# A decode attention and gMLP kernel under one critical section: recorded waits, a TensorE loop over 28 quads, one identity load per 16 matmuls

## The chip, the cores and the metric

The kernel runs on one core of a Trainium2 chip (trn2). The metric is device time in microseconds, in the median of several executions. Before the change it is 667.79 us, the median of three runs (667.62 to 667.85).

## The reference, cut to what matters

One decode step for four sequences (`B = 4`, one token each, width 512): adaLN modulation from `c`, cached attention with 32 heads of 128 over 4096 cached positions, and a gMLP block. Nearly all bytes are the two caches: 4 x 32 x 4096 x 128 values in bf16 each.

```python
mod = (silu(c) @ w_mod).reshape(4, 6, 1, 512)          # sa, ca, ga, sb, cb, gb
h = layernorm(x) * (1 + ca) + sa
q = (h @ wq) as [B, H, 1, 128]
p = softmax((q . k_cache) * 128**-0.5)                 # over 4096 positions
x = x + ga * ((p @ v_cache) as [B, 1, 4096] @ wo)
h = layernorm(x) * (1 + cb) + sb
z = gelu(h @ w_in); z1, z2 = halves of z; z2 = layernorm(z2)
x = x + gb * ((z1 * (w_sp * z2 + b_sp)) @ w_out)       # one token, so w_sp and b_sp are scalars
```

## The kernel before, in words

The work is cut into 32 quads, a quad being one batch and one group of four heads. A quad's K is one tile of 128 partitions x 16384 bf16 (4 MB), and so is its V. Partition 32 h + s holds 128 of the 4096 positions of head h.

The pool keeps two K tiles (`kt`) and two V tiles (`vt`). SyncE issues all large loads in one order that is written out by hand (lines 428 to 446): for quad i the K of quad i+1, every fourth quad half a megabyte of `wo_g`, and the V of quad i. A load of K into a buffer waits until the quad that used the buffer has been read by `scores`. A load of V waits for `values` in the same way. `w_mod` and `wq` use the two V buffers first. The last K comes in two pieces and the last V in five, and behind them stand `wo_l`, `win` and `wout`, the weights of the tail.

Per quad, in this order on the engines:

- `scores` (lines 272 to 285): VectorE multiplies each half of K by the broadcast query in place (L276), and TensorE sums over the 128 channels with 16 accumulating matmuls against the identity (L281). What is left are 8 partial sums per position in PSUM.
- `fold` (L290): VectorE adds the 8 partial sums.
- `softmax` (L298 to L319): VectorE finds each head's maximum with two 32 x 32 transposes, ScalarE takes the exponential (L311), and VectorE spreads it into `P4`, in which each partition's column of its head is filled and the other three are zero (L314).
- `values` of the quad before: 32 matmuls with `P4` as weights and V moving (L341); ScalarE copies the result out (L347), and `diagonal` (L354) picks the wanted blocks one quad later.
- `project` (L374, L375) divides by the sum, and `apply` (L391 to L400), every fourth quad, multiplies by that group's `wo`.

The last quad uses `values_last` (L363), 128 small matmuls with V as weights, whose pieces wait for the pieces of the last V. The tail (lines 471 to 545) follows: layer norm, `win` (L499), gelu, `wout` (L522), and 4 KB out.

Tile's framework places the waits, in a schedule in program order. All TensorE code is unrolled: 3024 weight loads and 3024 matmuls.

Of the kernel before, what the change touches and what calls it, by code (L numbers as in the profile page):

```python
# [8 lines left out]
BF16 = mybir.dt.bfloat16  # L9
# [3 lines left out]
AX = mybir.AxisListType  # L13


@with_exitstack
def kernel(
# [16 lines left out]
    nc = tc.nc  # L34
    ctx.enter_context(tc.manual_schedule())
# [12 lines left out]
    EL = HT * DH  # L48
    DC = 8
    assert J == 4 and DH == P and SK % R == 0 and HT * DC == 512 and FH % P == 0  # L50
    att_scale = float(DH) ** -0.5
    LN_EPS = 1e-5

    consts = ctx.enter_context(tc.tile_pool(name="consts", bufs=1))
    persist = ctx.enter_context(tc.tile_pool(name="persist", bufs=1))
    kvp = ctx.enter_context(tc.tile_pool(name="kv", bufs=1))
    wk = ctx.enter_context(tc.tile_pool(name="work", bufs=1))

    rows = persist.tile([2 * B, D], BF16, name="rows")
    nc.scalar.dma_start(out=rows[0:B], in_=c)
    nc.scalar.dma_start(out=rows[B:2 * B], in_=A_x.rearrange("b s d -> (b s) d"))
    nc.scalar.preload_act_table_set("natural_log_exp_and_others")
    wb_t = persist.tile([1, 2], BF16, name="wb_t")
    nc.gpsimd.dma_start(out=wb_t[:, 0:1], in_=B_w_sp[0:1, 0:1])
    nc.gpsimd.dma_start(out=wb_t[:, 1:2], in_=B_b_sp.rearrange("(a b) -> a b", b=1))


    def vslot(cols):  # L70
        return kvp.tile([P, cols], BF16, name="vt", bufs=2)

    wm = vslot(J * 6 * D)
    nc.sync.dma_start(out=wm, in_=w_mod.rearrange("(p j) n -> p (j n)", j=J))
    wm = wm.rearrange("p (j n) -> p j n", j=J)
    GW = NH * DH
    wq = vslot(J * G * GW)
    nc.sync.dma_start(out=wq, in_=A_wq.rearrange("(p j) n -> p (j n)", j=J))  # L78
    wq = wq.rearrange("p (j n) -> p j n", j=J)

    quads = [(g, b) for g in range(G) for b in range(B)]

    def kv_view(cache, i):
        g, b = quads[i]
        return cache[b, g * NH:(g + 1) * NH].rearrange("h (s n) d -> (h s) (n d)", s=R)

    def load(cache, i, tag, parts):
        t = kvp.tile([P, NT * DH], BF16, name=tag, bufs=2)
        a = 0
        for part in parts:  # L90
            b = a + NT * DH // part
            nc.sync.dma_start(out=t[:, a:b], in_=kv_view(cache, i)[:, a:b])  # L92
            a = b
        return t.rearrange("p (n d) -> p n d", d=DH)

    def load_k(i):
        return load(A_k_cache, i, "kt", (2, 2) if i == len(quads) - 1 else (1,))

    def load_v(i):
        return load(A_v_cache, i, "vt", (2, 4, 8, 16, 16) if i == len(quads) - 1 else (1,))  # L100

    NQ = len(quads)


    ident = consts.tile([P, P], BF16, name="ident")
    make_identity(nc, ident)
    ones_b = consts.tile([1, P], BF16, name="ones_b")
    nc.vector.memset(ones_b, 1.0)
    ones_f = consts.tile([P, P], F32, name="ones_f")
    nc.vector.memset(ones_f, 1.0)  # L110

    sel = consts.tile([P, 32], F32, name="sel")
    nc.vector.tensor_reduce(
        out=sel, in_=ident.rearrange("p (t m) -> p m t", m=32), axis=AX.X, op=ALU.add,
    )
    mean_d = consts.tile([P, P], F32, name="mean_d")
    nc.vector.memset(mean_d, 1.0 / D)
    mean_f = consts.tile([P, P], F32, name="mean_f")
    nc.vector.memset(mean_f, 1.0 / FH)
    eps = consts.tile([P, 1], F32, name="eps")  # L120
    nc.vector.memset(eps, LN_EPS)
    wide = consts.tile([P, 4 * P], BF16, name="wide")
    nc.gpsimd.memset(wide, 0.0)
    busy_ps = [None]

    def keep_busy(n):

        if busy_ps[0] is None:
            busy_ps[0] = psum_s.tile([P, 4 * P], F32, name="big", bufs=2)
        for _ in range(n):  # L130
            nc.tensor.matmul(busy_ps[0], lhsT=ident, rhs=wide, start=True, stop=True)

    NB = 3

    mask4 = consts.tile([P, NH], F32, name="mask4")
    nc.gpsimd.memset(mask4, 0.0)
    for hl in range(NH):
        nc.gpsimd.memset(mask4[hl * R:(hl + 1) * R, hl:hl + 1], 1.0)
    P4s, mxs = [], []
    for i in range(NB):  # L140
        t = consts.tile([P, NT + 4, NH], BF16, name=f"P4_{i}")
        nc.gpsimd.memset(t, 0.0)
        P4s.append(t)
        t = consts.tile([P, R], F32, name=f"mx_{i}")
        nc.gpsimd.memset(t, 0.0)
        mxs.append(t)
# [4 lines left out]
    def ln_stats(pool, psum, buf, ones, n, name, meanwhile=None):  # L151

        nc.vector.tensor_tensor(out=buf[:, 1], in0=buf[:, 0], in1=buf[:, 0], op=ALU.mult)
        ps = psum.tile([P, 2, n, B], F32, name="small", bufs=1)
        nc.tensor.matmul(
            ps.rearrange("p s j b -> p (s j b)"), lhsT=ones,
            rhs=buf.rearrange("p s j b -> p (s j b)"), start=True, stop=True,
        )
        if meanwhile is not None:
            meanwhile()  # L160
        st = pool.tile([P, 2, B], F32, name=f"st_{name}")
        nc.vector.tensor_reduce(
            out=st, in_=ps.rearrange("p s j b -> p s b j"), axis=AX.X, op=ALU.add,
        )
        msq = pool.tile([P, B], F32, name=f"msq_{name}")
        nc.vector.tensor_tensor(out=msq, in0=st[:, 0], in1=st[:, 0], op=ALU.mult)
        var = pool.tile([P, B], F32, name=f"var_{name}")
        nc.vector.tensor_tensor(out=var, in0=st[:, 1], in1=msq, op=ALU.subtract)
        rstd = pool.tile([P, B], F32, name=f"rstd_{name}")
        nc.scalar.activation(out=rstd, in_=var, func=AF.Ln, bias=eps)  # L170
        nc.scalar.activation(out=rstd, in_=rstd, func=AF.Exp, scale=-0.5)
        return st[:, 0], rstd


    modT = persist.tile([P, 6, J, B], F32, name="modT")
    qbc = persist.tile([P, B, G, DH], BF16, name="qbc")
    x1b = persist.tile([P, 2, J, B], F32, name="x1b")
    wbf = persist.tile([P, 2], F32, name="wbf")
    xcT = persist.tile([P, J, 2 * B], F32, name="xcT")
    cT, x4T = xcT[:, :, 0:B], xcT[:, :, B:2 * B]  # L180
    xT = persist.tile([P, J, B], F32, name="xT")


    gwb = persist.tile([P, J, 3, B], F32, name="gwb")
    sT = persist.tile([P, J, B], BF16, name="sT")
    hbc = persist.tile([P, J, B, R], BF16, name="hbc")
    psum_acc = ctx.enter_context(
        tc.tile_pool(name="psum_acc", bufs=1, space=bass.MemoryType.PSUM)
    )
    attn_ps = psum_acc.tile([P, J, B], F32, name="attn_ps")  # L190
    psum_s = ctx.enter_context(
        tc.tile_pool(name="psum_s", bufs=1, space=bass.MemoryType.PSUM)
    )

    def mod_part(oc):
        ps = psum_s.tile([P, J, B], F32, name="small", bufs=1)
        for jo in range(J):
            c0 = oc * D + (jo if oc < 2 else jo * P)
            cols = slice(c0, c0 + (P - 1) * J + 1, J) if oc < 2 else slice(c0, c0 + P)
            for j in range(J):  # L200
                nc.tensor.matmul(
                    ps[:, jo, :], lhsT=wm[:, j, cols],
                    rhs=sT[:, j, :], start=(j == 0), stop=(j == J - 1),
                )
        if oc in (1, 4):
            nc.vector.tensor_scalar_add(out=modT[:, oc], in0=ps, scalar1=1.0)
        else:
            nc.vector.tensor_copy(out=modT[:, oc], in_=ps)

    def query(b, g0, n, qp):  # L210

        for j in range(J):
            wv = wq[:, j, :].rearrange("p (g h d) -> p g h d", h=NH, d=DH)
            for hl in range(NH):
                nc.tensor.matmul(  # L215
                    qp[hl * R:(hl + 1) * R, 0:n], lhsT=hbc[:, j, b, :],
                    rhs=wv[:, g0:g0 + n, hl, :],
                    start=(j == 0), stop=(j == J - 1),
                    tile_position=(0, hl * R),
                )  # L220

    with tc.tile_pool(name="pre", bufs=1) as pre:
        xc_ps = psum_s.tile([P, J, 2 * B], F32, name="small", bufs=1)
        for j in range(J):
            nc.tensor.matmul(
                xc_ps[:, j, :], lhsT=rows[:, j::J],
                rhs=ident[0:2 * B, 0:2 * B], start=True, stop=True,
            )
# [24 lines left out]
        for oc in range(2, 6):  # L253
            mod_part(oc)
# [321 lines left out]
```

## Time and profile before

| | |
|---|---|
| median of three runs | 667.79 us (667.62 to 667.85) |
| span of the profiled execution, first to last instruction | 665.5 us |
| what lies around the span, as the difference of the two | 2.3 us |
| busy: TensorE, its weight loads, VectorE, ScalarE | 415.7, 204.6, 402.6, 41.3 us |
| moved by DMA | 283.17 MB, mean 426 GB/s |
| mean granted TensorE clock | 0.771 of full speed |

The profiled execution has no time of its own beside its span, so the difference to the median stands for what lies around it. The page gives busy times of engines, the span in 40 slices, the DMA queues, the chain that ended last, and groups of instructions with their idle time. `PEld` is the weight load of TensorE, `SPq` a DMA issue by SyncE. The queue of kind "hardware_dynamic" carries the loads, and the queues of kind "instruction" carry the engines' own code.

The packed trace has every DMA packet with its start, duration, size and queue. A load of 128 partitions is dealt out over 16 DMA engines, eight partitions each, and every engine closes its share with a 4-byte packet. Sixteen such packets close one load. Their spread shows how far the engines have drifted apart.

### The profile page before, as it was taken

What the parts mean: (1) busy time and instruction counts of PE and PEld (TensorE: products, weight loads), DVE (VectorE), ACT (ScalarE), POOL (GpSimd) and SP (SyncE); (2) the same over time, 40 slices, a digit from 0 to 9 for tenths busy, and PEclk for the clock granted to TensorE, in tenths of its full rate; (3) what the DMA queues carried; (4) which work ended last, traced back from release to release, by engine and by line L of the source; (5) the groups of instructions that cost most, each with busy time, mean ns of one, the idle gap of its engine ahead of it and who ended that gap; (6) DMA issues with size and microseconds to landing.
All of it is one profiled execution on the core that took longest, in us unless ns stands there. A gap on an engine that the chain in (4) does not pass through costs nothing.

```text
span 665.5 us, 6939 instructions
## 1 busy us (share of the span) xinstructions
PE 415.7 (62%) x3024; PEld 204.6 (31%) x3024; DVE 402.6 (61%) x475; ACT 41.3 (6%) x115; POOL 4.7 (1%) x21
## 2 busy tenths in 40 slices
PE   2557776655677655676555477654657655657775
PEld 2223333222333322233222233232223322223334
DVE  2166776675556576547666456666555666655762
ACT  1200000000000000000000000000000000000002
POOL 2000000000000000000000000000000000000000
PEclk9977777668887667887667788676888766888795
DMA  9999999999999999999999999999999999999995
GB/s 379 439 425 427 437 439 424 429 438 434 427 428 441 428 428 434 435 426 434 433 436 424 436 435 430 423 439 435 428 431 435 433 430 432 437 426 435 428 417 236
DMA packets 12749, 283.17 MB, mean 426 GB/s; under 512 B 1448, under 2 KB 1968, under 8 KB 4016
## 3 DMA queue, kind: packets, MB, share of 16 engines
q1 hardware_dynamic: 12640, 282.73, 98.9%
q8 instruction: 23, 0.38, 0.2%
q14 instruction: 6, 0.05, 0.0%
q0 software_dynamic: 64, 0.00, 0.0%
q10 hardware_dynamic: 16, 0.01, 0.0%
HBM read 282.73 MB, written 0.00 MB: 425 GB/s over the span
## 4 chain that ended last, share of the span: by engine, by line
DMA 62%; PE 24%; DVE 12%; issue 0%; SPq 0%; ACT 0%; DVEq 0%
DMA kt<-in_A_k_cache_dram 58%; PE s_ps L281 24%; DVE kt L276 11%; DMA vt<-in_A_v_cache_dram 3%; DMA wout_437<-in_B_w_out_dram 1%; PE big L341 0%; DVE S L290 0%; ACT E L311 0%; SPq L92 0%; DVE P_1_109 L314 0%; DVE P_0_105 L314 0%; PE y_ps L522 0%; DVE nm L308 0%; DVE mT L300 0%; SPq L78 0%
## 5 line engine op out<-in xcount | busy, mean ns | idle before, releaser
L281 PE MATMUL s_ps<-kt,ident 128*128 128x512 bf16 x1024 | 293.5, 457 | 185.5 <-DVE kt L276 185.5
L276 DVE TENSOR_TENSOR kt<-kt,qbc 128x8192 bf16<-128x8192 bf16 x64 | 282.7, 4420 | 82.9 <-DMA kt<-in_A_k_cache_dram 82.9
L281 PEld LDWEIGHTS <-ident 128*128 128x128 bf16 x1024 | 116.4, 114 | 351.1 <-issue 229.8
L290 DVE TENSOR_REDUCE S<-s_ps 128x64 f32<-128x512 f32 x64 | 44.3, 692 | 125.5 <-PE s_ps L281 125.5
L354 PE MATMUL zo_ps<-sel,osb 128*128 128x4 f32 x248 | 33.2, 257 | 26.6 <-ACT osb L347 26.6
L311 ACT ACTIVATE E<-S,nm 128x128 f32<-128x128 f32 x32 | 12.8, 401 | 563.4 <-DVE nm L308 563.4
L354 PEld LDWEIGHTS zo_ps<-sel,osb 128*128 128x128 f32 x248 | 30.6, 194 | 38.4 <-ACT osb L347 38.4
L341 PE MATMUL big<-vt,P_0_105 128*32 128x512 bf16 x352 | 21.0, 380 | 1.5 <-DMA vt<-in_A_v_cache_dram 1.5
L341 PE MATMUL big<-vt,P_1_109 128*32 128x512 bf16 x320 | 19.1, 380 | 0.0
L341 PE MATMUL big<-vt,P_2_113 128*32 128x512 bf16 x320 | 19.1, 380 | 0.0
L347 ACT COPY osb<-big 128x512 f32<-128x512 f32 x31 | 17.6, 566 | 20.0 <-PE big L341 20.0
L215 PE MATMUL big<-vt,hbc 128*32 128x512 bf16 x128 | 9.6, 471 | 5.2 <-DMA vt<-in_A_wq_dram 5.2
L314 DVE TENSOR_TENSOR P_1_109<-E,mask_99 128x512 bf16<-128x512 f32 x11 | 7.6, 692 | 6.8 <-ACT E L311 6.8
L314 DVE TENSOR_TENSOR P_0_105<-E,mask_99 128x512 bf16<-128x512 f32 x11 | 7.6, 692 | 6.7 <-ACT E L311 6.7
L341 PEld LDWEIGHTS <-P_0_105 128*32 128x32 bf16 x352 | 8.4, 96 | 8.9 <-DMA vt<-in_A_v_cache_dram 1.6
L314 DVE TENSOR_TENSOR P_2_113<-E,mask_99 128x512 bf16<-128x512 f32 x10 | 6.9, 692 | 6.2 <-ACT E L311 6.2
L400 PE MATMUL attn_ps<-oP,wo_g 128*128 128x4 bf16 x112 | 3.8, 164 | 10.6 <-DVE oP L397 10.6
L341 PEld LDWEIGHTS <-P_1_109 128*32 128x32 bf16 x320 | 7.6, 96 | 6.7
L341 PEld LDWEIGHTS <-P_2_113 128*32 128x32 bf16 x320 | 7.6, 96 | 6.7
L375 DVE TENSOR_TENSOR oT<-zo_ps,rz 128x4 bf16<-128x4 f32 x32 | 5.4, 168 | 7.1 <-PE zo_ps L363 6.0
L215 PEld LDWEIGHTS <-hbc 128*32 128x32 bf16 x128 | 4.4, 114 | 10.3 <-issue 8.4
L308 DVE STREAM_TRANSPOSE nm<-hb 128x32 f32<-128x32 f32 x32 | 6.8, 212 | 1.1
(221 smaller groups left out, 131.1 us busy)
## 6 DMA issues: line engine op xcount, KB each, us to landing
kt<-in_A_k_cache_dram SPq DMA_DIRECT2D x31, 4096.0 KB, 26.0
vt<-in_A_v_cache_dram SPq DMA_DIRECT2D x31, 4096.0 KB, 33.7
vt<-in_A_wq_dram SPq DMA_DIRECT2D x1, 4096.0 KB, 20.4
kt<-in_A_k_cache_dram SPq DMA_DIRECT2D x2, 2048.0 KB, 24.8
wo_g<-in_A_wo_dram SPq DMA_DIRECT2D x7, 512.0 KB, 26.5
vt<-in_w_mod_dram SPq DMA_DIRECT2D x1, 3072.0 KB, 9.8
vt<-in_A_v_cache_dram SPq DMA_DIRECT2D x1, 2048.0 KB, 17.8
win_434<-in_B_w_in_dram SPq DMA_DIRECT2D x1, 1344.0 KB
```

What stands on the lines that cost most here:

```text
L215: nc.tensor.matmul(qp[hl * R:(hl + 1) * R, 0:n], lhsT=hbc[:, j, b, :], rhs=wv[:, g0:g0 + n, hl, :], start=(j == 0), stop=(j == J - 1), til ...
L276: nc.vector.tensor_tensor(out=kt, in0=kt, in1=q[:, None, :].to_broadcast([P, HT, DH]), op=ALU.mult,)
L281: nc.tensor.matmul(ps, lhsT=ident, rhs=kt[:, :, cc * DC:(cc + 1) * DC], start=(cc == 0), stop=(cc == DH // DC - 1),)
L290: nc.vector.tensor_reduce(out=st["S", i][:, half * HT:(half + 1) * HT], in_=st.pop(("s", i, half)), axis=AX.X, op=ALU.add,)
L308: nc.vector.transpose(out=nm, in_=hb)
L311: nc.scalar.activation(out=E, in_=S, func=AF.Exp, bias=nm[:, 0:1], scale=att_scale, accum_out=rs,)
L314: nc.vector.tensor_tensor(out=P4[:, 0:NT, :], in0=E[:, :, None].to_broadcast([P, NT, NH]), in1=mask4[:, None, :].to_broadcast([P, NT, NH]) ...
L341: nc.tensor.matmul(po[32 * t:32 * t + 32], lhsT=P4[:, n0:n0 + 8, :], rhs=st["v", i][:, n0:n0 + 4, :], start=(u == 0), stop=(u == NU - 1), ...
L347: nc.scalar.copy(out=osb, in_=po)
L354: nc.tensor.matmul(st["o", i], lhsT=osb[:, n, :], rhs=sel[:, NH * n:NH * n + NH], start=(n == 0), stop=(n == 3),)
L375: nc.vector.tensor_tensor(out=oT[:, :, b], in0=st.pop(("o", i)), in1=rz, op=ALU.mult,)
L400: nc.tensor.matmul(attn_ps[:, jo, :], lhsT=(wo_g[:, hl] if g < G - 1 else wo_l[hl // 2][:, hl % 2])[:, jo * P:(jo + 1) * P], rhs=oT[:, hl, :],
```

## The change

The kernel is written anew around a small recorder. Each instruction is recorded with its engine and the regions that it reads and writes. From these the recorder works out which earlier instruction of another engine (or DMA) each one must wait for, and leaves out what an earlier wait has already covered. Tiles are allocated by hand. Then everything is emitted inside one `tile_critical` section with semaphores of its own.

- TensorE's code of quads 2 to 29 is emitted once, as four quads in a loop of seven passes. Inside the loop TensorE waits only on semaphores named `pe_...`, and at the end of each pass it takes off them what the pass has added. The other engines stay unrolled.
- In `scores` the identity is loaded once per 16 matmuls (`mm2`, then `moving`). The tail's products with `wo_l`, `win` and `wout` also have separate weight loads.
- `P4`, `mx`, `S` and `rs4` have two buffers where there were three; `wo_g`, `oT` and `oP` have one where there were two. The load of `wo_g` moves from the first quad of a group to the third, still ahead of that quad's V.
- The two scalars `w_sp` and `b_sp` are loaded from ScalarE's queue and not from GpSimd's. The last large loads still wait for the load eight places before.

```diff
+class Program:
+    def add(self, eng, emit, reads, writes, sem=None, done=True, dma=False, after=()):
...
+        op.deps = self.depend(op) | set(after) | set(lst[-2:-1] if eng == "POOL" else ())
...
+    def run(self, alloc, passes, engines):
...
+        def emit(op, eng, waits):
+            waits = list(waits)
+            for s, v in waits[1:]:
+                eng.wait_ge(sems[s], v)
+            inst = op.emit(eng)
+            if waits:
+                inst._wait_ge(sems[waits[0][0]], waits[0][1])
+            if op.done:
+                inst.then_inc(sems[op.sem], 16 if op.dma else 1)
...
+        with pe.Fori(0, passes):
+            for op, w in zip(loops[0], norm):
+                emit(op, pe, w.items())
+            for s in sorted(own):
+                if step[s]:
+                    pe.sem_inc(sems[s], -step[s])
...
+    def mm2(out, lhsT, rhs, start, stop, done=False):
+
+        prog.add("PE", lambda e: e.ldweights(lhsT), [lhsT], [], done=False)
+        moving(out, lhsT, rhs, start, stop, done)
+
+    def moving(out, lhsT, rhs, start, stop, done=False):
+        def emit(e):
+            return e.add_instruction(mybir.InstMatmult(
...
+                tile_size=(P, P), tile_position=(0, 0), ldweights=False,
...
     def scores(i, half):
...
-                nc.tensor.matmul(
-                    ps, lhsT=ident, rhs=kt[:, :, cc * DC:(cc + 1) * DC],
-                    start=(cc == 0), stop=(cc == DH // DC - 1),
+            (mm2 if cc == 0 else moving)(
+                s_ps[half], ident, kh[:, :, cc * DC:(cc + 1) * DC], cc == 0, cc == n - 1, cc == n - 1,
...
+    def load_sp(sem, out, in_):
+        near_end = sem[:2] in ("wo", "wi")
+        sp_dma.append(prog.load("SP", sem, out, in_, after=sp_dma[-8:-7] if near_end else ()))
...
+    PASSES = (NQ - 4) // B
+
+    load_k(0)
+    for i in range(NQ):
+        prog.passno = (i - 2) // B if 2 <= i < 2 + B * PASSES else None
+        g, b = divmod(i, B)
+        if i + 1 < NQ:
+            load_k(i + 1)
+        if b == 2 and g < G - 1:
+            load_sp("pe_wo", wo_g, wo_w[g])
+        load_v(i)
...
+    with tc.tile_critical():
...
+        prog.run(alloc, PASSES, {
+            "PE": nc.tensor, "DVE": nc.vector, "ACT": nc.scalar, "POOL": nc.gpsimd, "SP": nc.sync,
+        })
+        nc.sync.wait_ge(sems["out"], 16)
```

## The prediction

> **What bounds the kernel now.** I read the page's slices and queues first, then the groups, the waits, the DMA issues, the last 14 us of the DMA view, the timeline of the tail, and at last the trace's single packets. The page:
>
> ```profile
> DMA  9999999999999999999999999999999999999995
> ...
> q1 hardware_dynamic: 12640, 282.73, 98.9%
> q8 instruction: 23, 0.38, 0.2%
> q14 instruction: 6, 0.05, 0.0%
> ```
>
> The DMA engines are never idle until the last slice. TensorE (62%) and VectorE (61%) wait in turns, as the groups show:
>
> ```profile
> L281 PE MATMUL s_ps<-kt,ident 128*128 128x512 bf16 x1024 | 293.5, 457 | 185.5 <-DVE kt L276 185.5
> L276 DVE TENSOR_TENSOR kt<-kt,qbc 128x8192 bf16<-128x8192 bf16 x64 | 282.7, 4420 | 82.9 <-DMA kt<-in_A_k_cache_dram 82.9
> L281 PEld LDWEIGHTS <-ident 128*128 128x128 bf16 x1024 | 116.4, 114 | 351.1 <-issue 229.8
> ```
>
> TensorE waits for VectorE's product, VectorE for K. The DMA issues (KB each, us to landing):
>
> ```profile
> kt<-in_A_k_cache_dram SPq DMA_DIRECT2D x31, 4096.0 KB, 26.0
> vt<-in_A_v_cache_dram SPq DMA_DIRECT2D x31, 4096.0 KB, 33.7
> ```
>
> By the packets a 4 MB load keeps each of the 16 DMA engines busy for 9.68 us, so 16 us (K) and 24 us (V) of earlier loads stand ahead of a new one: a later issue costs nothing until that is used up. The end looks different, in the DMA view of 648 to 662 us (40 slices):
>
> ```profile
> DMA  9999999999999999999999786555655454410000
> GB/s 398 389 407 417 398 398 435 399 407 399 416 404 395 440 385 429 389 440 420 413 417 446 322 313 233 227 231 231 262 222 240 202 202 176 176 61 0 0 0 0
> ```
>
> From 656 to 660.6 us about half of the engines work: nearly half of the bandwidth is lost for 4.6 us. Every load has the same share on every engine, so some engines lag. The closing packets of single loads show it, in ns after the fastest engine's:
>
> ```
>  load closing at   9.5 us: 0 163 169 203 312 326 363 389 425 437 460 514 574 596 614 634
>  load closing at 216.6 us: 0 163 169 312 326 425 574 614 1304 1618 1785 1810 1858 1929 2010 2054
>  load closing at 608.8 us: 0 168 326 574 614 744 1162 2975 3039 3147 3342 3428 4627 4639 4696 4895
> ```
>
> Between two loads these numbers stand still to the nanosecond, except on one engine at a time, at known moments. After each of q8's 23 packets of 16 KB one engine is 1.42 us later for good (437 to 1858, 634 to 2054, 389 to 1809, ...). They come when TensorE has started 220, 476, 709, ..., 5878 weight loads and matmuls, 257 apart: its own code, 64 bytes an instruction. They go round eight engines in turn: the first, ninth and seventeenth hit the same one (437, 1858, 3278, 4694). So the worst has three: 635 + 3 x 1420 = 4895 ns. The q14 packets of 8 KB at 66.9, 238, 434.2 and 617.9 us come when VectorE has started 59, 179, 310 and 431 instructions. The first three took one engine outside those eight from 460 to 1304, 2150 and 2975, some 840 each; with the fourth it ends near 3830.
>
> A load lands when its slowest engine is done, and the tail is paced by that:
>
> ```profile
> 657.81 1.08 PE L499 MATMUL z_ps<-h,win_434 128*128 128x4 bf16 x30 [1.75 <-DVE h L486]
> 660.26 0.57 PE L522 MATMUL y_ps<-u,wout_436 128*128 128x12 bf16 x16
> 660.93 0.40 PEld L522 LDWEIGHTS <-wout_437 128*128 128x128 bf16 x12 [0.18 <-DMA wout_437<-in_B_w_out_dram]
> ```
>
> The last product's weights wait 0.18 us for `wout`; the arithmetic before it follows the last pieces of V within 0.1 to 0.9 us. All of this shifts with the slowest engine, one for one.
>
> **The change, part by part.**
>
> *The loop.* By the listing of the changed kernel, one pass is about 540 TensorE instructions: four quads of 16 `diagonal`, 34 `scores` and 68 sum and `values`, 64 of `apply`, a few semaphores. About 610 stand before it, 730 after: 1,880 in place of 6,048. At 256 per packet that is 7 refills, if the passes fetch nothing again. Seven hit seven engines once: worst 635 + 1420 = 2055 ns, a gain of 2.84 us. But VectorE stays unrolled with the same 475 operations, so its engine keeps 3830, and 3830 becomes the worst: the gain is 4.895 - 3.83 = **1.07 us**. If passes do fetch again, 610 + 7 x 540 + 730 = 5,120 instructions cross 20 blocks, and a jump back may fetch one more per pass: 20 to 27 refills, three or four per engine: 0 to -1.42 us. No row shows a jump. I take the first case: eight engines in turn look like eight places for a block, 2,048 instructions, and a pass fills two or three.
>
> [...]
>
> *The identity.* 960 of the 1024 loads of 114 ns go. They lie under the matmuls: 16 of L281 in full clock take 3.61 us, 226 ns each, while a load is under way beside them. Between 0 and 30 x 114 ns = 3.4 us per quad; I take near 0. Either way VectorE's 82.9 us of waiting for K hide it. If K did not come last, it would be worth that much. What it brings earlier is an issue of K into a full queue.
>
> *Buffers and issues.* `P4` and `S` with two buffers wait for `values` two quads back, done a quad earlier: 0. `wo_g` now waits for the last `apply` (16 matmuls, a copy on VectorE waited for 1.5 us, 16 more), and SyncE holds that quad's V behind it; I bound the delay by 0 and 6 us, against 24 us queued. Tightest is the ramp:
>
> ```profile
> 45.07 0.33 SPq L92 DMA_DIRECT2D kt<-in_A_k_cache_dram  x1
> ```
>
> That is the third K. The fastest engine ends what is queued at 49.5 us, in the changed kernel 1.26 us earlier because `wo_g` has gone from there: 48.2. An issue takes 1.1 us to its first packet (0.75 to 1.85 at the start), so 46.2: the margin is 2.0 us. Ahead of it stand the first K, L276 and 32 matmuls, as before: 0, and beyond 2.0 us every microsecond would count. The two scalars' loads now stand ahead of ScalarE's table load, at 0.26 to 0.68 us an issue; the table was there at 2.9 us and is first used at 8.1, so 0. GpSimd, rid of them, has the identity some 1.2 us earlier, and the first matmul waits for `rows` until 7.8 us anyway.
>
> *The tail.* The last quad's reciprocal now waits for all of `values_last`, since the sum has no signal of its own: one more VectorE operation, 0.17 us, before `apply`. There TensorE waits 0.29 and 0.30 us for the two pieces of `wo_l`, which covers it. Without that cover: +0.2.
>
> *Entry and exit.* The critical section adds a meeting of all engines at each end.
>
> ```profile
> SPq L571 <- DMA out_dram<-ot: 0.7, 1, 0.7
> SPq L571 <- PEq L571: 0.6, 2, 0.5
> ```
>
> Two such meetings cost 0.6 us here; Tile's closing waits go. Bounds -0.3 and +1.2; I take +0.25, one short meeting at each end less some waits.
>
> *Sum.* The span becomes 665.5 - 1.07 + 0.25 = 664.7. What lies around the span (2.3 us to the median of 667.79) stays: 667.79 - 0.82 = 666.97, **667.0 us**.
>
> **The rivals.**
>
> 1. *VectorE's code does not hold the end* (its hits fall on several engines, or fewer fall). For it: single q14 packets at 238 and 336.6 us hit other engines. Against: three hits in a row on one. Worst 2055: 667.79 - 2.84 + 0.25 = 665.2.
> 2. *The loop does not do what it says*: code is fetched at every block as before. Three hits: 668.0; four: 669.5. For it: packets came exactly at block ends, whatever was held.
> 3. *Slower: the passes' refetches fall on the same engines*, a block of code being tied to its engine. For it: the strict round of eight. A pass spans three blocks, so three engines get seven hits each: 635 + 7 x 1420 = 10.6 us, 5.7 more than now: 673.7. It decides from the fourth hit on one engine. Against: the round may simply count.
>
> That the DMA engines run dry through a new wait I hold below one in thirty; past the 2.0 us margin it costs the excess.
>
> **How the numbers follow.** Main case 0.55, rivals 0.13, 0.20 and 0.12. A difference of 0.2%, 1.34 us, is about what a measurement of this kernel can tell from no change: faster means below 666.45, slower above 669.1. The main case reaches from 666.1 (VectorE's engine with three hits, 2.99) to 667.9 (entry and exit at +1.2); a quarter of it, 0.14, is below 666.45. Faster: 0.13 + 0.14 = 0.27. Same: 0.41 + 0.13 of rival 2 = 0.54. Slower: 0.07 + 0.12 = 0.19. The range takes rivals 1 and 2 in, 665.2 to 669.5, and leaves rival 3 out. The main case alone: 666.1 to 667.9.
>
> **What would show it.** Right: q8 with about 7 packets, q14 still about 6; the half-empty stretch of DMA at the end shorter by about 1 us, one engine left for its last microsecond; L281 with 64 weight loads; VectorE still waiting for K. Wrong: q8 with 20 or more packets (rival 2 if the end is as before, rival 3 if a few engines run alone for 10 us), an end without a laggard (rival 1), or a slice before the last with a DMA digit below 9.

## The result, and the profile after

The changed kernel takes 670.23 us (median of 5, 670.11 to 670.27), the kernel before, run on the same chip, 667.62 us (667.41 to 667.85): ratio 1.0039, 95% interval 1.0027 to 1.0051. It is slower by 2.6 us, by more than measurement leaves open, where 0.8 us less was forecast. The profiled execution has a span of 668.3 us (before 665.5).

The page after, the lines of the DMA engines and their queues:

```profile
DMA  9999999999999999999999999999999999999995
...
q1 hardware_dynamic: 12640, 282.73, 98.8%
q8 instruction: 7, 0.11, 0.1%
q14 instruction: 6, 0.05, 0.0%
```

The DMA engines are as full as before and carry the same 282.73 MB. TensorE's code comes in 7 packets in place of 23, VectorE's and the others' 6 are still there: the loop does what it says. Its groups:

```profile
L360 PE MATMUL bank<-kt,ident 128*128 128x512 bf16 x1024 | 295.0, 459 | 180.9 <-DVE kt L136 180.9
L136 DVE TENSOR_TENSOR kt<-kt,qbc 128x8192 bf16<-128x8192 bf16 x64 | 282.7, 4420 | 86.6 <-DMA kt<-in_A_k_cache_dram 86.6
L355 PEld LDWEIGHTS <-ident 128*128 128x128 bf16 x64 | 9.1, 142 | 359.4 <-issue 359.3
```

64 identity loads in place of 1024, the same matmuls and the same product, and VectorE waits for K longer, 86.6 us against 82.9. K comes later, and no engine is the reason. The end, first by the DMA view of 648 to 662 us (40 slices), then by the timeline:

```profile
DMA  9898999999999999999999999999999765431000
GB/s 492 328 462 345 369 392 392 421 354 380 376 351 397 361 407 360 429 398 395 382 402 369 423 401 408 429 389 407 411 395 410 296 268 214 171 135 61 23 23 29
```

```profile
662.58 0.57 PE L360 MATMUL bank<-u,wout 128*128 128x12 bf16 x16
663.32 0.40 PEld L355 LDWEIGHTS <-wout 128*128 128x128 bf16 x12 [0.26 <-DMA wout<-in_B_w_out_dram]
...
665.45 0.36 SPq L729 DMA_DIRECT2D out_dram<-ot  x1
```

The half-empty stretch that began at 656 us begins at 659 and is steeper: at 660.4 us a third of the engines work, from 661 us one. Fewer engines lag, as forecast. But the whole picture lies later; `out` is issued 2.3 us later than before.

The single packets of the trace say why. Each 4 MB load is 128 packets of 32 KB, one row of K or V each. Between 60 and 620 us, those that a code packet falls on (over 1300 ns) left out:

```
             packets   mean ns   exactly 1213 ns   the fastest engine closes the load at
before        7247     1213.00       99.9%             618.52 us
after         7251     1217.13       17.4%             620.90 us
```

The same bytes of the same two tensors take 4.1 ns longer per packet, 8 packets per engine and load: over 64 loads 8 x 64 x 4.13 ns = 2.1 us. The first loads (before 20 us) are at 1213 ns in both. What the change moved for these packets is where they are written: in the built program K and V begin at bytes 121600, 154368, 56064 and 88832 of each partition before, at 16512, 49280, 82048 and 114816 after. The first four are multiples of 256, the last four are 128 past one: the change puts all tiles into one pool, with K and V first.

The exit is longer too. SyncE's waits after:

```profile
SPq L733 <- DMA out_dram<-ot: 1.0, 1, 1.0
SPq L769 <- PEq L769: 0.8, 2, 0.6
```

0.7 and 0.6 us before. From the issue of `out` to the end of the span it is 2.87 us, before 2.31.

### The profile page after: what moved, and what is told of

The parts are those of the page before. It is cut to its first block, busy times and chain, and to the rows that moved or that the text cites. A ratio compares the mean times of both kernels' runs of the same rounds, so it can differ in the third digit from the quotient of the medians.

```text
span 668.3 us, 5909 instructions
## 1 busy us (share of the span) xinstructions
PE 420.4 (63%) x3024; PEld 94.2 (14%) x2065; DVE 402.9 (60%) x475; ACT 41.3 (6%) x115; POOL 3.2 (0%) x17
## 3 DMA queue, kind: packets, MB, share of 16 engines
q1 hardware_dynamic: 12640, 282.73, 98.8%
HBM read 282.73 MB, written 0.00 MB: 423 GB/s over the span
## 4 chain that ended last, share of the span: by engine, by line
DMA 63%; PE 24%; DVE 12%; issue 0%; SPq 0%; ACT 0%; DVEq 0%
DMA kt<-in_A_k_cache_dram 58%; PE bank L360 23%; DVE kt L136 11%; DMA vt<-in_A_v_cache_dram 3%; DMA wout<-in_B_w_out_dram 1%; PE bank L349 0%; SPq L141 0%; DVE S L136 0%; DVE P L136 0%; ACT E L136 0%; DVE mx L136 0%; DVE nm L136 0%; DVE mT L136 0%; DVE hm L136 0%; DVE hb L136 0%
## 5 line engine op out<-in xcount | busy, mean ns | idle before, releaser
L360 PE MATMUL bank<-kt,ident 128*128 128x512 bf16 x1024 | 295.0, 459 | 180.9 <-DVE kt L136 180.9
L136 DVE TENSOR_TENSOR kt<-kt,qbc 128x8192 bf16<-128x8192 bf16 x64 | 282.7, 4420 | 86.6 <-DMA kt<-in_A_k_cache_dram 86.6
L136 DVE TENSOR_REDUCE S<-bank 128x64 f32<-128x512 f32 x64 | 44.3, 692 | 125.6 <-PE bank L360 125.6
L355 PEld LDWEIGHTS <-ident 128*128 128x128 bf16 x64 | 9.1, 142 | 359.4 <-issue 359.3
L349 PE MATMUL bank<-vt,P 128*32 128x512 bf16 x992 | 59.2, 380 | 0.5 <-DMA vt<-in_A_v_cache_dram 0.5
L349 PE MATMUL bank<-sel,osb 128*128 128x4 f32 x248 | 35.7, 267 | 29.4 <-ACT osb L136 25.0
L349 PEld LDWEIGHTS bank<-sel,osb 128*128 128x128 f32 x248 | 33.0, 207 | 41.9 <-ACT osb L136 36.9
L136 DVE TENSOR_TENSOR P<-E,mask 128x512 bf16<-128x512 f32 x32 | 22.2, 693 | 18.0 <-ACT E L136 18.0
L349 PEld LDWEIGHTS bank<-rs,ones_f 128*128 128x128 f32 x64 | 12.1, 190 | 104.8 <-issue 104.0
L349 PEld LDWEIGHTS bank<-vt,P 128*32 128x32 bf16 x992 | 23.6, 96 | 21.4 <-DMA vt<-in_A_v_cache_dram 0.6
L136 ACT COPY osb<-bank 128x512 f32<-128x512 f32 x31 | 17.5, 565 | 17.4 <-PE bank L349 17.3
```

The source lines that it names most:

```text
L136: eng, lambda e: getattr(e, name)(*args, **kw), ins, outs, sem=sem, done=done, after=after,
L349: "PE", lambda e: e.matmul(out, lhsT=lhsT, rhs=rhs, start=start, stop=stop, **kw),
L355: prog.add("PE", lambda e: e.ldweights(lhsT), [lhsT], [], done=False)
L360: return e.add_instruction(mybir.InstMatmult(name=nc.get_next_instruction_name(), engine=mybir.EngineType.PE, ins=[e.lower_ap(rhs), e.lowe ...
```

## The experiments

Theory A: the place of K and V in SBUF makes the loads slower. Theory B: something in the new order (loop, semaphores, fewer weight loads) disturbs them. Each experiment was timed beside the kernel before on the same chip. The kernel before took 667.35 us beside the first four, 667.64 (one run) beside the next four and 667.39 beside the last four. Differences below are to that. The lag of a DMA engine is how much later than the fastest engine's its closing packet of a load comes; the pace is the time from load to load on the fastest engine.

**1. The changed kernel with K and V back on multiples of 256.**

```diff
+    pad = sb.tile([P, 64], BF16, name="pad")
     kt = tile2([P, NT * DH], BF16, "kt")
```

> The changed kernel with an unused tile of 128 bytes per partition ahead of the K and V tiles, which moves every tile that follows by 128 bytes: K and V begin at 256 past a multiple of 512, as in the kernel before, in place of 128 past. The traces show 32 KB packets of K and V of 1213 ns before and 1217.5 ns (mean) after the change. Theory A (the place of K and V in SBUF makes the packets longer): packets back at 1213 to 1214 ns, 64 loads of 4 MB each 0.03 us shorter, 2.1 us less than the changed kernel: 668.1 us. Theory B (the load in the loop, the semaphores or the order of VectorE and TensorE disturb the transfers): packets stay at 1217 to 1218 ns and the time at 670.2 us.

667.13 us (11 runs), 0.22 us less than before: ratio 0.9997, 0.9988 to 1.0006. Packets 1213.00 ns. 128 unused bytes give back 2.8 us (+2.61 to -0.22). The pace shows in the table of stretches, 60 to 620 us (last column: GB/s), of the changed kernel:

```profile
60.00:620.00 560.00, 355.79 (x2347) 72.86 (x1499) 352.46 (x383) 27.96 (x87) 0.00 (x0) 0.76 1.00 431
```

and of this one:

```profile
60.00:620.00 560.00, 355.49 (x2352) 73.04 (x1499) 355.00 (x383) 27.94 (x87) 0.00 (x0) 0.76 1.00 433
```

Equal work on the engines, DMA share 1.00 in both, and yet 431 against 433 GB/s: a busy share can't show this. The end, 648 to 662 us:

```profile
DMA  9999999999999999999999997444210000000000
GB/s 421 395 398 372 426 397 418 417 423 399 380 402 415 392 437 389 401 410 411 408 410 401 401 414 291 173 195 173 76 41 23 26 26 18 0 0 0 0 0 0
```

The changed kernel's shape, earlier: the last data land at 659.82 us (before 660.61, changed 662.83). Theory A is right, and its price was too low: the expected 2.1 us are the pace alone, 620.90 - 618.85 = 2.05 us as measured; the rest is the slowest engine's lag (3.71 us at 619 us, in the changed kernel 4.28 at 621) and the small last pieces.

**2. The kernel before with K and V moved off.**

```diff
     kvp = ctx.enter_context(tc.tile_pool(name="kv", bufs=1))
+    pad = kvp.tile([P, 64], BF16, name="pad")
```

> The kernel before with the same unused tile of 128 bytes ahead of its K and V tiles, which then begin at 384 past a multiple of 512 in place of 256; nothing else differs. Theory A: packets longer than 1213 ns, by up to the 4.5 ns of the changed kernel, and 1 to 2 us more than the kernel before: 668.8 to 669.8 us. Theory B: 1213 ns and 667.6 us.

670.24 us, +2.89: ratio 1.0042, 1.0029 to 1.0056. Packets 1216.99 ns, 22% of them at 1213. No loop, no critical section, and the whole loss. (`wo_g` and `wo_l` stand in the same pool and move off with K and V.) The product's wait grows as in the changed kernel:

```profile
L277 DVE TENSOR_TENSOR kt<-kt,qbc 128x8192 bf16<-128x8192 bf16 x64 | 282.7, 4420 | 86.9 <-DMA kt<-in_A_k_cache_dram 86.9
```

The time is above the 669.8 expected, since not only the pace suffers: a packet on which code falls takes up to 1876 ns in place of 1764, so that the lag of the slowest engine at the end is 5.5 us in place of 4.9.

**3. The passes written out.**

```diff
-        with pe.Fori(0, passes):
-            for op, w in zip(loops[0], norm):
-                emit(op, pe, w.items())
...
+        for op in self.by_eng["PE"]:
+            if op.pos >= first:
+                emit(op, pe, plain(op))
```

> The changed kernel with TensorE's seven passes written out, in place of the loop; the identity is still loaded once per 16 matmuls. Some 5,080 TensorE instructions in place of 1,880 from the chip's point of view: 19 or 20 instruction packets on q8 in place of 7, which in the kernel before hit eight engines in turn for 1.42 us each. Theory A (the loop is worth what the prediction said, and the packets' 1217.5 ns come from the place in SBUF): 19 or 20 hits make the worst lag 635 + 3 x 1420 = 4.9 us in place of about 4.2 us, 0.7 to 1.1 us slower than the changed kernel: 671.0 us, packets still 1217.5 ns. Theory B (the loop itself lengthens the packets): 1213 ns again, 2.1 us less for that and 0.7 to 1.1 us more for the refills: 668.9 us.

670.99 us, +3.64: ratio 1.0055, 1.0041 to 1.0069. Packets 1216.89 ns: the loop is not what lengthens them.

```profile
q8 instruction: 20, 0.33, 0.2%
```

20 packets of code; at 621 us the slowest engine is 5.1 us behind the fastest, 4.3 with the loop. Against the changed kernel 3.64 - 2.61 = 1.0 us (by the two times themselves 0.8).

**4. The identity loaded each time.**

```diff
-            (mm2 if cc == 0 else moving)(
+            mm2(
```

> The changed kernel with the identity loaded for each of the 16 matmuls of the q.k sums again, 30 loads more per quad; the loop stays. The prediction put the loads under the matmuls and under VectorE's wait for K: the time of the changed kernel within 0.3 us, 670.2 us, VectorE's wait for K shorter by at most 3.4 us per quad. Theory A: packets 1217.5 ns as in the changed kernel. A rival (fewer weight loads let TensorE read K from SBUF more densely, against the writes of the loads): packets nearer to 1213 ns and up to 2.1 us less, 668.1 us.

670.19 us, +2.84: ratio 1.0041, 1.0028 to 1.0055; the span is 668.4 us, changed kernel 668.3. Packets 1217.08 ns.

```profile
L136 DVE TENSOR_TENSOR kt<-kt,qbc 128x8192 bf16<-128x8192 bf16 x64 | 282.7, 4420 | 84.4 <-DMA kt<-in_A_k_cache_dram 84.4
L355 PEld LDWEIGHTS <-ident 128*128 128x128 bf16 x1024 | 118.6, 116 | 350.3 <-issue 276.4
```

109.5 us more of weight loading cost nothing that shows (+2.84 here, +2.61 in the changed kernel); VectorE's wait is 2.2 us shorter over the whole kernel, 0.07 us per quad.

**5. Loads with almost no engine at K and V.** The product takes `kh[:, 0:1, :]` alone, the sums take 2 matmuls of 16 from that one row, `values` 2 groups of 8 from four rows of V.

> The changed kernel (K and V at 128 past a multiple of 512) with almost no engine access to K and V: VectorE multiplies one of the 128 rows of 128 in each half, TensorE sums that row over and over in 2 matmuls of 16, and the sums over V read the first four rows in 2 groups of 8. All loads stay. Left out is most of the product and of the sums. The time goes by the loads alone. Theory A1 (the place of the bytes alone makes a packet longer): packets stay at 1217 to 1218 ns. Theory A2 (it takes engines that read and write K and V beside the loads: in the changed kernel's trace the packets of 19.5 to 36 us, before the first product, were 1213.0 to 1213.6 ns, and reached 1218 only from 53 us on): packets at 1213 to 1214 ns.

670.18 us (one run; +2.5), packets 1217.13 ns: theory A1. The engines are nearly idle in the groups,

```profile
L136 DVE TENSOR_TENSOR kt<-kt,qbc 128x128 bf16<-128x128 bf16 x64 | 14.0, 221 | 409.8 <-DMA kt<-in_A_k_cache_dram 409.8
```

and the time is the changed kernel's. So engines that read and write K and V beside the loads have no part in the longer packets, and the kernel is paced by its loads all the way. The late onset in the changed kernel, which spoke for A2, is there without compute too.

**6 to 8. Which places are good.** The pad of experiment 1 with 384, 448 and 160 bytes.

> The changed kernel with 384 unused bytes per partition ahead of K and V, which then begin at a multiple of 512. If what matters is a start at a multiple of 256: packets of 1213 ns, 667.1 us as with 128 unused bytes. If it is 256 past a multiple of 512 itself that is good: 1217 ns and 670.2 us.

> The changed kernel with 448 unused bytes ahead of K and V, which then begin at 64 past a multiple of 512. If a start at a multiple of 256 is what matters: 1217 to 1219 ns and 670.2 us, as at 128 and 384 past. If 64 past is good enough: 1213 ns and 667.1 us.

> The changed kernel with 160 unused bytes ahead of K and V, which then begin at 288 past a multiple of 512 (32 past a multiple of 64). If every start off a multiple of 256 costs the same: 1217 to 1219 ns and 670.2 us. If the price grows as the start is less round: longer packets than 1219 ns and more than 670.5 us.

One run each, beside those above (packets that code falls on left out):

```
K begins at   past a multiple of 256   mean ns   time us (to before)
  16640             0  (exp. 1)        1213.00   667.13 (-0.22)
  16896             0  (exp. 6)        1213.00   667.12 (-0.5)
  16512           128  (changed)       1217.13   670.23 (+2.61)
 121728           128  (exp. 2)        1216.99   670.24 (+2.89)
  16960            64  (exp. 7)        1216.95   670.36 (+2.7)
  16672            32  (exp. 8)        1217.92   670.63 (+3.0)
```

Among the places tried, a multiple of 256 is what counts; odd or even multiples are alike, and how far off a start lies hardly matters. 32 past adds 0.8 to 1.0 ns to what 64 and 128 past cost; by one run, that is no firm step in time.

**9. The loop alone.** Experiments 1 and 3 together.

> The changed kernel with 128 unused bytes ahead of K and V (packets of 1213 ns) and the seven passes written out in place of the loop: the loop alone, measured with K and V where they were before the change. By the prediction's step the loop saves 1.07 us, so this is 1.07 us slower than the run with 128 unused bytes and the loop: 668.2 us, with 20 packets on q8 and a worst lag near 4.9 us in place of 3.7. If the loop's gain in the pair without unused bytes (0.76 us) was all there is: 667.9 us. If the loop hides nothing: 667.1 us.

668.28 us, +0.89: ratio 1.0014, 1.0005 to 1.0023. Against experiment 1 that is 0.89 + 0.22 = 1.11 us; the slowest engine's lag at 619 us makes 0.91 of it (4.62 us against 3.71). The end, 648 to 662 us, is the one of before again, with half of the engines at work for 2.5 us and a few after:

```profile
DMA  9999999999999999999999998655655632120200
GB/s 433 360 421 386 417 397 424 398 411 401 385 427 398 430 398 436 398 459 372 379 417 370 373 376 331 265 209 236 246 198 236 240 140 79 70 79 26 47 0 0
```

**10. K on a multiple of 256, V off.** A second pad of 128 bytes between `kt` and `vt`.

> 128 unused bytes ahead of K and another 128 ahead of V: K begins at a multiple of 256 as in the kernel before, V at 128 past one. If each misplaced load costs the same, half of the loads pay: K's packets 1213 ns, V's 1217 to 1218 ns, mean 1215.3 ns, 667.13 + 3.1 / 2 = 668.7 us. If the price is that of K alone (the product is written back into K's place): 667.1 us; if of V alone: 670.2 us.

668.37 us, +0.98: ratio 1.0014, 1.0004 to 1.0023. That is 1.2 us more than experiment 1, not the 1.55 expected, and the packets tell that each misplaced load does not cost the same: K's 1213.4 ns, V's 1214.2, mean 1213.8 without those that code falls on. Among V's loads those right behind `wo_g`, which lies off a multiple of 256 too (at byte 161760, 224 past), stand out: 1216.3 ns, and 1213.5 for the others. The fastest engine loses 0.36 us until 619 us (0.78 x 512 = 0.40), where both misplaced lose 2.05. The rest of the 1.2 us is the end: the lag is 4.27 us (3.71 in experiment 1), and the last data land at 661.04 us. In the changed kernel the load that ends at 19.5 us, misplaced like the others, still runs at 1213.0 ns, and the excess grows over the next four (to 58 us). Both look like something that builds up over misplaced loads and goes down in a well placed one; no run here shows what it is.

**11. All weights on multiples of 256.** `wo_g`, `wo_l`, `win` and `wout` right behind `vt`, with the pad.

> 128 unused bytes ahead of K and V, and the weights of the output projection and of the MLP right behind V, so that each of their buffers begins at a multiple of 256 too (in the run with 128 unused bytes they begin at 32 past a multiple of 64). In that run the packets of 3072 bytes took 124.8 ns (121.0 in the kernel before), those of 3584 bytes 143.4 (141.0). 8 + 32 such packets per engine at the end: 8 x 3.8 + 32 x 2.4 = 0.1 us less at most: 667.0 us; 667.1 if the end does not follow.

666.88 us, -0.51: ratio 0.9993, 0.9984 to 1.0002. The 3072-byte packets are at 121.0 ns again, those of 3584 at 141.1. Right in direction, and too small to tell from nothing.

**12. Fewer VectorE instructions.**

```diff
-        dve("tensor_scalar_mul", out=rs4_t[i % 2], in0=mask4, scalar1=rs, sem="pe_dve")
+        act("activation", out=rs4_t[i % 2], in_=mask4, func=AF.Copy, scale=rs, sem="pe_act")
...
-        fold(i, 0)
-        fold(i, 1)
+        if i < NQ - 1:
+            dve("tensor_reduce", out=S_t[i % 2],
+                in_=s_all.rearrange("p (n d) -> p n d", d=DC), axis=AX.X, op=ADD)
+        else:
+            fold(i, 0)
+            fold(i, 1)
```

> The kernel of the run with all buffers at multiples of 256, and 63 VectorE instructions less: the two folds of a quad are one (but for the last quad), and the mask times the row sum is ScalarE's. VectorE has 412 instructions in place of 475; its packets of code came at 51.4, 218.2, 433.2 and 616.9 us or thereabouts, the fourth after some 430 instructions, so one of four falls away, of 0.84 us on one DMA engine. Theory (the end follows the slowest DMA engine): worst lag 2.9 us in place of 3.7, 0.8 us less than the kernel with all buffers at multiples of 256: 666.2 us, 1.1 us less than the kernel before. Rival (the later fold of a quad's first half delays the last quads, or another engine is as late): 667.0 us.

666.37 us, 1.02 us less than the kernel before: ratio 0.9985, 0.9976 to 0.9994, faster than both kernels.

```profile
q14 instruction: 5, 0.04, 0.0%
```

One packet of code less; at 619 us the slowest engine is 2.85 us behind in place of 3.57 in experiment 11. Data end 0.78 us earlier (658.98 us), but the kernel gained 0.5. The timeline tells where the rest went:

```profile
658.62 0.68 PE L353 MATMUL bank<-z2b,mean_f 128*128 128x56 f32 x2 [0.51 <-DVE z2b L136]
...
659.09 0.94 PE L364 MATMUL zob<-u,wout 128*128 128x12 bf16 x28
```

The last product no longer waits for `wout`; the 28 matmuls run through, and the arithmetic ahead of them is late next. In part that is this edit's own doing. It puts two banks of PSUM into one tile, `s_all`, and the recorder takes an access to a PSUM tile as one to its whole length: the gelu of one half now waits for both halves of the product with `win`. The two timelines show it, experiment 11 first:

```profile
656.97 1.92 PE L361 MATMUL bank<-h,win 128*128 128x4 bf16 x56 [1.73 <-DVE h L136]
658.36 0.20 ACT L136 ACTIVATE z2b<-bank 128x28 f32<-128x28 f32 x1 [0.63 <-PE bank L361]
```

```profile
656.19 1.92 PE L364 MATMUL s_all<-h,win 128*128 128x4 bf16 x56 [1.73 <-DVE h L136]
658.15 0.19 ACT L136 ACTIVATE z2b<-s_all 128x28 f32<-128x28 f32 x1 [1.20 <-PE s_all L364]
```

The gelu started 0.53 us before the end of the product; now it starts 0.04 us after it.

## Why the prediction was wrong, point by point

- *Refills by the loop: right.* 7 packets on q8. The worst lag with K and V in place is 3.71 us (experiment 1), forecast 3.83, with VectorE's four hits as what remains. The loop is worth 1.11 us (experiments 1 and 9; 1.0 by the other pair), forecast 1.07. Passes two to seven fetched nothing: no packet on q8 between 119.3 and 627.9 us. So the jump back over some 540 instructions brought no packet; how long a pass may be for that, no run shows. Rivals 2 and 3 fall. So does rival 1: in experiment 1 VectorE's fourth packet, at 617 us, takes the one slowest engine from 2.88 to 3.71 us, and the next engine stands at 2.24.
- *Identity: right.* Experiment 4: nothing that shows.
- *Buffers and issues, 0: the step that failed.* It followed waits, queues and margins, and they held: the DMA line has no digit below 9 before the last slice. It never asked where the buffers come to lie. One pool in place of several moved K and V by half of 256 bytes: +2.05 us of pace, and 0.57 us more lag for the slowest engine (4.28 at 621 us against 3.71). With K and V kept in place (experiment 1) the kernel takes 0.22 us less than before. The forecast was 0.82 less; what is missing is mostly the next term. That its 667.13 us lie so near to the forecast 667.0 is luck: the kernel before took 667.35 beside it, and the forecast started from 667.79. No rival had this mechanism either; the one on the slower side was that of refetched code.
- *Entry and exit, +0.25: too small by 0.53 us, within its bounds.* SyncE's first issue is 0.22 us later (0.75 to 0.97 us), and issue of `out` to end 0.56 us longer: 0.78 us. The prediction had counted one short meeting at each end, less some of Tile's waits. No run takes the section away, so this is read from the traces alone.
- *Tail, 0: right.* From the last data to the issue of `out` 2.62 us, before 2.55.

The sum as measured, from before to after: start and pace 620.90 - 618.52 = +2.38 (0.25 of it the start, by the first packet), lag 4.28 - 4.89 = -0.61, the last small pieces +0.45 (what is left of the 2.22 us by which the data end later), tail +0.07, exit +0.56: 2.85 us, the difference of the spans.

What the runs show of the failed step is the place alone: on average, packets were longer at every start tried off a multiple of 256 bytes (table of experiments 6 to 8). The price does not follow how far off the start lies: at 128, 64 and 32 past, the packets were 4.13, 3.95 and 4.92 ns longer. Why a misplaced packet is longer stays open.

## What to carry to other kernels

A change that moves tiles between pools, or their order in one, moves the destinations of all loads: list their places before and after, and try the large ones on multiples of 256 bytes per partition, the good places here: a pad of 128 bytes was worth 2.8 us of 670. Where DMA paces a kernel, compare the time of one packet of the main load (here 1213.00 and 1217.13 ns); the busy share was 1.00 either way. When the end follows the slowest DMA engine, instruction counts have a price too: a loop on TensorE brought 1.1 us, and one code packet less of VectorE half a microsecond, until arithmetic was late. Part of that lateness the edit made itself: one tile in place of two let the gelu wait for both.

## What the runs showed of the hardware

- A 32 KB packet into SBUF took 1213 ns at a start on a multiple of 256 bytes (before, experiments 1 and 6), and 1217 to 1218 ns on average at 32, 64 or 128 past (experiments 8, 7, 2 and the changed kernel); the first misplaced loads were not slower yet (1213 ns before 20 us in the changed kernel), and with K well placed and V not, V's took 1214.2 (1216.3 right behind a misplaced `wo_g`, 1213.5 otherwise; experiment 10).
- A TensorE loop body of some 540 instructions ran its second to seventh pass without a fetch (no packet on q8 between 119.3 and 627.9 us); with the identity loads in it (some 660, experiment 4) one packet more came in all, 8 in place of 7.
- A packet on which a fetch of code fell took up to 1764 ns with K and V on multiples of 256 (before), up to 1876 off them (experiment 2).
